# Half of one batch's x turned by VectorE and SBUF transfers instead of TensorE, the last tile in three pieces, a new order of the work

## The chip, the cores and the metric

The kernel runs on one core of a Trainium2 chip. The metric is the device time of one execution in microseconds (us), as the median of several runs. Beside it stands one execution taken by the hardware profiler, with its trace. Engines are called PE (TensorE; its weight loads PEld), DVE (VectorE), ACT (ScalarE), POOL (GpSimd) and SP (SyncE). DMAs are issued by SP or ACT, each in its own queue.

## What is computed

Causal attention for 4 batches of 8 heads over 768 tokens of 64 dimensions: three heads ("retrieval") see all earlier keys, five ("streaming") see the first 4 keys and a window of the last 64. The outputs of a batch's heads side by side are x (768 rows of 512), which goes through a feed-forward part with a maximum of two products.

```
scores = scale * q @ k.T, masked per head (full causal, or sink + window)
x      = softmax(scores) @ v                    # (4*768, 512)
g      = maximum(x @ w1, x @ w2)                # d_ff 1024
out    = g @ w_out                              # (3072, 512), float32
```

## The kernel before

The maximum is taken as relu(x·(w1−w2)) + x·w2, so that x needs one product with w12 = w1−w2 ("up"), and the output is x·(w2·w_out) plus relu(..)·w_out ("down"). The products with constant weights are made once at the start.

Attention goes by pairs of heads: 4 pairs a batch, 16 in all, numbered n. For a pair SP loads q, k and v (L478, L489); POOL casts them to bf16 (L423); q and k are turned by DVE in 32x32 squares (L566; the first pairs by PE, L552). PE makes scores (`ps`, L626), ACT takes their exponential (`at`, L643), DVE multiplies by a mask (L665), PE makes the weighted sums (`po`, L687), and DVE divides by the sum and writes x (L702, L704). x of one batch is 768 rows in 6 blocks of 128; "half" 0 is the first three blocks and half 1 the others.

Before the feed-forward part x has to be turned so that its 512 columns lie on partitions (`xt`). There are two ways. For batches 0, 1 and 2 (counting from 0), PE turns 12 blocks of 128x128 a half into a bank of PSUM (`px`, L720), and ACT or DVE copies them out (`take_x`, L748). For batch 3 (`SQUARES_FROM`, L364), DVE turns all 32x32 squares of a half in one instruction (`turn_x_squares`, L730, into `xs`), and 16 DMAs a half from SBUF to SBUF put the squares where they belong (`regroup_x`, L742); SP issues 8 of them and ACT 8.

The feed-forward part of a batch runs in two groups of three blocks: 8 "ups" of 4 matmuls (`ph`, L761), whose relu is taken by ACT (L772) or DVE (L774), then 3 "downs" of 12 matmuls (`pout`, L788), copied out (L421 on ACT, L423 on DVE) and stored (L836). The last tile of all is split in two column halves of 256 (`down_columns`, L803; `give_columns`, L815): the first is copied out by DVE and stored by SP, the second is copied and stored by ACT.

The order of the instructions on every engine is set before the program runs. A planner (`Order.plan`) has all operations with a cost and what they depend on, and plays them through. PE takes from lists in a fixed priority: x transposes (TX), scores (S), weighted sums (W), turns of q and k (TQ), feed-forward (F), products of weights (P) and, until 33 us, empty matmuls that keep PE busy (D, L903). Inside F the order is fixed: all of a batch's group 0, then group 1, then the next batch. The other engines and SP's queue take, of what is ready, the operation of the lowest rank: loads have rank 0, copies out of PSUM and late stores −1, attention of pair n about n, and `regroup_x` of batch 3 has n plus 4 for half 1. A list of seeds (`SEEDS`, `vary`) shifts the ranks of a few operations at random for each seed; PE's operations are not shifted.

Of the kernel before, what the change touches and what calls it, by code (L numbers as in the profile page):

```python
# [12 lines left out]
F32 = mybir.dt.float32  # L13
# [3 lines left out]
ACT = mybir.ActivationFunctionType  # L17
# [93 lines left out]
def heads_of(slots):  # L111
# [17 lines left out]
    130124, 130127, 130134, 130135, 130145, 130154, 130184, 130208, 130320, 130381, 130399, 130452,  # L129
    130492, 130575, 130609, 130687, 130849, 131260, 131273, 131785, 131855, 131967, 132048, 132807,  # L130
    220218, 220306, 220334, 220390, 220446, 220561, 220818, 222814, 223249, 223552, 223658, 223665,
)


class Op:


    def __init__(self, engine, cost, emit, deps=(), rank=0, tail=0.12, bank=False, issue=0.55, by="SP", single=False, port=False, shy=False):
        self.cost = cost if isinstance(cost, dict) else {engine: cost}
        self.engine, self.emit, self.rank, self.tail = engine, emit, rank, tail  # L140
        self.deps, self.bank = [d for d in deps if d is not None], bank
        self.issue, self.by, self.single, self.port, self.shy = issue, by, single, port, shy
        self.end, self.ready, self.users = None, 0.0, []
        self.behind, self.followers = None, []


class Order:
# [44 lines left out]
    def vary(self, seeds):  # L192

        self.link()
        movable = [o for o in self.ops if o.engine != "PE"]
        for seed in seeds:
            rng = random.Random(seed)
            for o in rng.sample(movable, rng.choice((1, 2, 4, 8, 20))):
                o.shift = o.shift + rng.gauss(0, 2.0) if rng.random() < 0.8 else 0.0
# [149 lines left out]
def tile_paired_heads(tc, q, k, v, w1, w2, wo, out, qkf, vf, tab, idle, heads):  # L349

    nc = tc.nc
    B, H, S, D = q.shape
# [8 lines left out]
    GTILES = GT // 128  # L361
    scale = 1.0 / float(D) ** 0.5
    ident, smask, causal = tab[:, 0:128], tab[:, 128:896], tab[:, 896:1024]
    TURNED, ANY_CASTS, SQUARES_FROM = 5, HP, B - 1  # L364
    RANKS, W_RANK = 1.0, 2.0
    FRONT = "B00 B01 B02 B03 B04 A0 L10 L11 w0 L12 w1 B10 B11 B12 B13 B14 A1 w2 w3 o0 o1 o2 o3"
    FIRST_LANDS, FIRST_TAKES = (6.0, 8.5, 12.1), (2.45, 2.55, 3.5)
# [45 lines left out]
    T = {}  # L413

    def in_bank(shape, dtype, name):

        return banks[order.bank].tile(shape, dtype, tag="b", name=name)
# [305 lines left out]
    def turn_x_squares(b, half):  # L723


        def emit(_):
            if half == 0:
                T["xs", b] = xs_pool.tile([128, NB, d_model], BF16, tag="xs", name="xs")
            rows = slice(3 * half, 3 * half + 3)
            nc.vector.transpose(  # L730
                T["xs", b][:, rows].rearrange("p i f -> p (i f)"),
                T["x", b][:, rows].rearrange("p i h d -> p (i h d)"),
            )
        return emit
# [55 lines left out]
                )  # L790
        return emit

    def down_columns(b, i, side):
        tg, ti = divmod(i, GTILES)
        cols = slice(d_model // 2 * side, d_model // 2 * side + d_model // 2)

        def emit(_):
            pout, g = in_bank([128, d_model // 2], F32, "pout"), T["g", b, tg]
            T["pout", b, i, side] = pout
            steps = [(xts[b % len(xts)][:, i, kc, :], w2o[:, kc, cols]) for kc in range(KC)]  # L800
            steps += [(g[:, fc, ti * 128:(ti + 1) * 128], wob[:, fc, cols]) for fc in range(FC)]
            for e, (lhsT, rhs) in enumerate(steps):
                nc.tensor.matmul(  # L803
                    pout, lhsT=lhsT, rhs=rhs, start=(e == 0), stop=(e == len(steps) - 1)
                )
        return emit

    def give_columns(b, i, side):
        cols = slice(d_model // 2 * side, d_model // 2 * side + d_model // 2)
        r0 = b * S + i * 128  # L810

        def emit(e):
            ot = outp.tile([128, d_model // 2], F32, tag="half", name="ot")
            copy(e, ot, T["pout", b, i, side])
            dma["ACT" if e == "ACT" else "SP"].dma_start(out=out[r0:r0 + 128, cols], in_=ot)  # L815
        return emit


# [94 lines left out]
    def prepare_w(c, rank):  # L913
        loaded = load(W_TAKES[c][0], load_w2(c), tail=W_TAKES[c][1])
        old, frees = take("qn")
        T["w1f", c] = slot("qn")[:, 0:KC * 256].rearrange("p (c f) -> p c f", c=KC)
        o = load(W_TAKES[c][2], load_w1(c), old, tail=W_TAKES[c][3])
        for two in range(2):
            subs[c, two] = op(
                None, {"DVE": 0.69, "POOL": 1.27}, subtract(c, two), [o, loaded], rank=rank, port=True, shy=True,  # L920
            )
            frees.append(subs[c, two])
        cast = op(None, {"DVE": 0.7, "POOL": 1.05}, cast_w2(c), [loaded], rank=rank, port=True)
        w2_casts.append(cast)
        ev = op(None, {"DVE": 0.69, "ACT": 1.05}, take_w2(c), rank=rank)
        ev.deps = [pe("P", 0.6, turn_w2(c), [cast], bank=ev)]
        w2t_ops.append(ev)

    def rank_of(n, part):
# [111 lines left out]
    def weigh(n, half, rank):  # L1041
        b, p = divmod(n, HP)
        mine = [x for x in tiles if used(n, x, half) and x in mask_ops]
        if (p, half) == (0, 0):
            done_with["x", b] = take("x")
        norm = op("DVE", 0.97, normalise(n, half), [*done_with["x", b][0]], rank=rank)
        for x in mine:
            w = pe(
                "W", len(used(n, x, half)) * 0.031 + 0.03,
                weighted(n, x, half, x == mine[0], x == mine[-1]),  # L1050
                [*mask_ops[x], *v_ready[n]], bank=norm if x == mine[0] else False,
            )
            frees_at[x].append(w)
        norm.deps.append(w)
        norms[b, half].append(norm)
        done_with["v", n][1].append(w)
        if (p, half) == (HP - 1, 0):
            done_with["xt", b] = take("xt")
        if p == HP - 1 and b >= SQUARES_FROM:
            if half == 0:  # L1060
                done_with["xs", b] = take("xs")
            o = op("DVE", 1.78, turn_x_squares(b, half), [*norms[b, half], *done_with["xs", b][0]], rank=n)
            done_with["x", b][1].append(o)
            turned.setdefault(b, []).append(o)
            whole = b < B - 1
            if half == 1 or not whole:
                rows = slice(0 if whole else 3 * half, 3 * half + 3)
                moved = [
                    op(
                        "DMA", 0.5 if whole else 0.25, regroup_x(b, rows, g, a),  # L1070
                        [*turned[b], *done_with["xt", b][0]], rank=n + 4 * half, issue=0.66,
                        by=("SP", "ACT")[a % 2], tail=1.2,
                    ) for g in range(4) for a in range(4)
                ]
                done_with["xs", b][1].extend(moved)
                for h in (0, 1) if whole else (half,):
                    x_ready[b, h] += moved
        elif p == HP - 1:
            for blocks in ((0, 1), (2,)) if half == 0 else ((3, 4), (5,)):
                m = len(blocks)  # L1080
                ev = op(None, {"DVE": 0.1 + 0.29 * m, "ACT": 0.2 + 0.4 * m}, take_x(b, blocks), rank=-1)
                o = pe("TX", 0.24 * m, turn_x(b, blocks), norms[b, half], bank=ev)
                ev.deps = [o, *done_with["xt", b][0]]
                done_with["x", b][1].append(o)
                x_ready[b, half].append(ev)
# [70 lines left out]
    def downs(b, tg):  # L1156
        for i in range(tg * GTILES, tg * GTILES + GTILES):
            if (b, i) == (B - 1, NB - 1):
                for side in range(2):
                    ev = op("DVE" if side == 0 else "ACT", 0.4, give_columns(b, i, side), rank=-1)  # L1160
                    ev.deps = [pe(
                        "F", 1.3, down_columns(b, i, side), [*w2o_ops, *relus[b, tg]], bank=ev
                    )]
                continue
            old, frees = take("ot") if b >= PARKED else ([*subs.values(), *w2_casts], [])
            ev = op(None, {"DVE": 0.68, "ACT": 0.6}, take_out(b, i), old, rank=-1)
            for part in range(3):
                o = pe(
                    "F", 0.87, down(b, i, part), [*w2o_ops, *(relus[b, tg] if part else ())],
                    bank=ev if part == 0 else False,  # L1170
                )
            ev.deps = [o, *ev.deps]
            done_with["xt", b][1].append(o)
            frees.append(op("DMA", 0.66, store(b, i), [ev], rank=N if b < PARKED else -1))
# [589 lines left out]
```

## Time and profile before

| | us |
|---|---|
| median of 3 runs | 183.93 |
| the 3 runs | 181.79, 183.93, 184.63 |
| the profiled execution | 181.13 |
| its span (first to last instruction) | 179.3 |
| PE busy | 171.5 |
| DVE busy | 113.5 |
| ACT busy | 110.7 |
| POOL busy | 59.2 |

The span is what the views below divide; some 1.8 us of the profiled execution lie outside it. Busy times overlap each other. The granted clock of TensorE is 0.999 over the span. A wait in these views is named by the semaphore that came last.

### The profile page before, as it was taken

The page shows a single profiled execution, that of the slowest core. Times are in us where ns is not written, and L with a number is a line of the kernel's source. Part 1 is how long each engine was busy: PE and PEld are TensorE (multiplying, and loading weights), DVE is VectorE, ACT ScalarE, POOL GpSimd, SP SyncE. Part 2 cuts the span into 40 slices and gives each one's busy share as a digit, 9 for nine tenths or more (in the row PEclk, how much of TensorE's full clock was granted, in tenths as well). Part 3 has the DMA queues.
Part 4 walks back from the last instruction along what each step waited for, and adds up shares of the span by engine and source line. Part 5 has one row for each costly group of instructions (what it writes and reads, how often), then busy time and mean ns, then how long its engine had stood idle before and what let it go on. Part 6 is the DMA issues. An engine that isn't in the chain of part 4 may idle for free.

```text
span 179.3 us, 4746 instructions
## 1 busy us (share of the span) xinstructions
PE 171.5 (96%) x1682; PEld 96.9 (54%) x1682; DVE 113.5 (63%) x270; ACT 110.7 (62%) x168; POOL 59.2 (33%) x98
## 2 busy tenths in 40 slices
PE   6899999999999999999999999999999999999990
PEld 1265665666455554556555656556555545545560
DVE  2578999871474899997979999999559530000000
ACT  3388999786767377598674896978634005426410
POOL 2244254704265655446545437535000000000000
PEclk9999999999999999999999999999999999999999
DMA  5999999989799899799897998999712668122032
GB/s 166 312 260 347 232 293 385 349 267 253 126 194 196 136 207 192 119 202 202 131 199 147 174 168 147 167 193 400 272 58 69 111 72 180 41 89 90 0 117 75
DMA packets 120675, 32.90 MB, mean 184 GB/s; under 512 B 107587, under 2 KB 116547, under 8 KB 120643
## 3 DMA queue, kind: packets, MB, share of 16 engines
q1 hardware_dynamic: 113954, 31.73, 76.4%
q10 hardware_dynamic: 6688, 0.79, 3.0%
q8 instruction: 15, 0.25, 0.6%
q14 instruction: 18, 0.14, 0.3%
HBM read 25.43 MB, written 6.29 MB: 177 GB/s over the span
## 4 chain that ended last, share of the span: by engine, by line
PE 77%; DMA 8%; DVE 7%; ACT 2%; issue 2%; POOL 1%; SPq 1%; POOLq 0%
PE pout L788 29%; PE ph L761 23%; PE ps L626 8%; PE po L687 6%; DMA w2f<-in_moe_w_dram 4%; PE po L868 4%; DMA qkf<-in_k_dram 4%; DVE at L665 2%; PE px L720 2%; DVE x L704 2%; ACT at L643 2%; PE ps L600 2%; PE pout L803 1%; DVE qk L566 1%; PE pt L552 1%
## 5 line engine op out<-in xcount | busy, mean ns | idle before, releaser
L643 ACT ACTIVATE at<-ps 128x1024 bf16<-128x1024 f32 (+2 forms) x64 | 59.5, 979 | 12.5 <-PE ps L626 9.4
L788 PE MATMUL pout<-wob,g 128*128 128x512 bf16 x184 | 45.2, 379 | 0.0
L761 PE MATMUL ph<-xt,w 128*128 128x384 bf16 x256 | 44.7, 326 | 0.0
L423 POOL CAST qb<-qkf 128x768 bf16<-128x768 f32 (+1 forms) x40 | 25.1, 643 | 35.1 <-DMA qkf<-in_k_dram 16.7
L761 PEld LDWEIGHTS <-w 128*128 128x128 bf16 x256 | 24.1, 98 | 15.6 <-issue 0.4
L772 ACT ACTIVATE g<-ph 128x384 bf16<-128x384 f32 x55 | 26.6, 492 | 8.8 <-PE ph L761 8.1
L665 DVE TENSOR_TENSOR at<-at,tab 128x1024 bf16<-128x1024 bf16 (+5 forms) x45 | 26.2, 609 | 8.8 <-ACT at L643 8.6
L788 PEld LDWEIGHTS <-g 128*128 128x128 bf16 x184 | 16.8, 98 | 18.5 <-issue 0.2
L704 DVE TENSOR_TENSOR x<-po,rez 128x192 f32 x64 | 22.9, 357 | 2.2
L788 PE MATMUL pout<-w2o,xt 128*128 128x512 bf16 x92 | 23.7, 379 | 0.0
L421 ACT COPY ot<-pout 128x512 f32<-128x512 f32 (+1 forms) x10 | 5.6, 563 | 27.5 <-PE pout L788 15.0
L687 PEld LDWEIGHTS <-at 128*128 128x128 bf16 x477 | 18.2, 98 | 6.4 <-issue 0.6
L626 PE MATMUL ps<-qk 64*128 64x128 bf16 (+2 forms) x307 | 21.2, 234 | 0.0
L566 DVE STREAM_TRANSPOSE qk<-qb 128x768 bf16<-128x768 bf16 x22 | 21.2, 966 | 0.0
L423 DVE COPY ot<-pout 128x512 f32<-128x512 f32 (+1 forms) x3 | 1.8, 603 | 30.5 <-PE pout L803 26.5
L687 PE MATMUL po<-vb,at 128*128 128x65 bf16 x387 | 20.7, 194 | 0.3 <-DVE at L665 0.3
L423 POOL CAST vb<-vf 128x768 bf16<-128x768 f32 (+1 forms) x18 | 12.2, 688 | 21.6 <-DMA vf<-in_v_dram 15.0
L626 PEld LDWEIGHTS <-qk 64*128 64x128 bf16 x307 | 11.6, 94 | 12.9 <-issue 9.6
L423 POOL COPY vx<-vb 64x650 bf16<-64x650 bf16 (+3 forms) x24 | 15.1, 632 | 1.7 <-DVE vb L423 0.5
L788 PEld LDWEIGHTS <-xt 128*128 128x128 bf16 x92 | 8.3, 98 | 8.7
L626 PE MATMUL ps<-qk,kx 64*128 64x128 bf16 x91 | 9.2, 216 | 0.1
L702 DVE RECIPROCAL rez<-po 128x6 f32<-128x6 f32 x32 | 5.9, 186 | 5.0 <-PE po L687 4.9
(67 smaller groups left out, 144.9 us busy)
## 6 DMA issues: line engine op xcount, KB each, us to landing
vf<-in_v_dram SPq DMA_DIRECT2D x24, 192.0 KB, 3.1
qkf<-in_q_dram SPq DMA_DIRECT2D x44, 96.0 KB, 3.4
qkf<-in_k_dram SPq DMA_DIRECT2D x44, 96.0 KB, 2.6
out_dram<-ot SPq DMA_DIRECT2D x11, 256.0 KB, 2.4
w2f<-in_moe_w_dram SPq DMA_DIRECT2D x4, 512.0 KB, 7.9
qkf<-in_moe_w_dram SPq DMA_DIRECT2D x4, 512.0 KB, 8.4
qkf<-in_moe_w_out_dram SPq DMA_DIRECT2D x4, 512.0 KB, 5.3
out_dram<-w2f SPq DMA_DIRECT2D x8, 256.0 KB, 3.5
```

The costliest lines, as they stand in the source:

```text
L423: eng[e].tensor_copy(out=out, in_=in_)
L566: nc.vector.transpose(T["qk", n][:, t], T["qb", n, 0][:, t])
L626: nc.tensor.matmul(ps[:, bank, e * 128:(e + wide) * 128], lhsT=lhsT, rhs=qk[rows, 0, i * 128:(i + wide) * 128], start=bank not in begun, s ...
L643: nc.scalar.activation(out=at[:, 0:len(w), 0:w[0]], in_=T["ps", n, t][:, 0:len(w), 0:w[0]], func=ACT.Exp, scale=scale,)
L665: eng[e].tensor_tensor(out=at, in0=at, in1=tbl, op=ALU.mult)
L687: nc.tensor.matmul(po[:, hh, b[-1] - 3 * half, :], lhsT=at[:, bank, e * 128:(e + 1) * 128], rhs=rhs, start=first and (bank, hh, e, b) == m ...
L702: nc.vector.reciprocal(out=rez, in_=po[:, :, :, D])
L704: nc.vector.tensor_tensor(out=T["x", b][:, 3 * half:3 * half + 3, bass.ds(heads[PLACES[n][hh]], 1), :], in0=po[:, hh, :, 0:D].unsqueeze(2) ...
L761: nc.tensor.matmul(ph, lhsT=w12[:, kc, fc * 128:(fc + 1) * 128], rhs=xts[b % len(xts)][:, 3 * tg:3 * tg + 3, kc, :], start=(kc == 0), stop ...
L772: nc.scalar.activation(out=g[:, fc, :], in_=ph, func=ACT.Relu)
L788: nc.tensor.matmul(pout, lhsT=lhsT, rhs=rhs, start=(e == 0), stop=(e == len(steps) - 1))
L868: nc.tensor.matmul(T["po2", kc], lhsT=w2t[:, fc, kc * 128:(kc + 1) * 128], rhs=wob[:, fc, :], start=(fc == 0), stop=(fc == FC - 1),)
```

## The change

The second half of batch 2 is turned in the way of batch 3: by DVE's squares and 16 DMAs. Those DMAs get rank −2, ahead of every load, copy and store, and all but the first of them are exempt from the seeds' shifts (`fixed`). The last tile's columns are made in three pieces, of 256, 128 and 128; DVE copies the first two and ACT the third, and SP issues all three stores. 30 seeds are added, and two costs in the planner (of `turn_w2` and of the regrouping DMAs) and the flag `fixed` feed the planner, so the order of the work on all engines is made anew.

```diff
@@ SEEDS
+    310092, 310174, 310178, 310206, 310265, 310282, 310350, 310385, 310535, 310648, 310677, 311155,
+    210002, 210008, 210033, 210047, 210079, 210081, 210089, 210160, 210255, 210282, 210367, 210423,
+    210770, 210861, 210874, 211140, 211669, 212024, 212690, 810963,
@@ Order.vary
-        movable = [o for o in self.ops if o.engine != "PE"]
+        movable = [o for o in self.ops if o.engine != "PE" and not o.fixed]
@@ tile_paired_heads
-    TURNED, ANY_CASTS, SQUARES_FROM = 5, HP, B - 1
+    TURNED, ANY_CASTS = 5, HP
+    SQUARES = ((B - 2, 1), (B - 1, 0), (B - 1, 1))
@@ turn_x_squares
-            if half == 0:
+            if ("xs", b) not in T:
@@ down_columns
-    def down_columns(b, i, side):
+    def down_columns(b, i, cols):
...
-            pout, g = in_bank([128, d_model // 2], F32, "pout"), T["g", b, tg]
+            pout, g = in_bank([128, cols.stop - cols.start], F32, "pout"), T["g", b, tg]
@@ give_columns
-            ot = outp.tile([128, d_model // 2], F32, tag="half", name="ot")
-            copy(e, ot, T["pout", b, i, side])
-            dma["ACT" if e == "ACT" else "SP"].dma_start(out=out[r0:r0 + 128, cols], in_=ot)
+            ot = outp.tile([128, d_model // 2], F32, tag="half", name="ot")[:, 0:cols.stop - cols.start]
+            copy(e, ot, T["pout", b, i, cols.start])
+            nc.sync.dma_start(out=out[r0:r0 + 128, cols], in_=ot)
@@ prepare_w
-        ev.deps = [pe("P", 0.6, turn_w2(c), [cast], bank=ev)]
+        ev.deps = [pe("P", 0.47, turn_w2(c), [cast], bank=ev)]
@@ weigh
-        if p == HP - 1 and b >= SQUARES_FROM:
-            if half == 0:
+        if p == HP - 1 and (b, half) in SQUARES:
+            if b not in turned:
                 done_with["xs", b] = take("xs")
             o = op("DVE", 1.78, turn_x_squares(b, half), [*norms[b, half], *done_with["xs", b][0]], rank=n)
...
-                        "DMA", 0.5 if whole else 0.25, regroup_x(b, rows, g, a),
-                        [*turned[b], *done_with["xt", b][0]], rank=n + 4 * half, issue=0.66,
-                        by=("SP", "ACT")[a % 2], tail=1.2,
+            moved = [
+                op(
+                    "DMA", 0.25, regroup_x(b, slice(3 * half, 3 * half + 3), g, a),
+                    [o, *done_with["xt", b][0]], rank=-2 if b < B - 1 else n + 4 * half, issue=0.66,
+                    by=("SP", "ACT")[a % 2], tail=1.2, fixed=b < B - 1 and g + a > 0,
+                ) for g in range(4) for a in range(4)
+            ]
@@ downs
-                for side in range(2):
-                    ev = op("DVE" if side == 0 else "ACT", 0.4, give_columns(b, i, side), rank=-1)
+                for first, m in ((0, 256), (256, 128), (384, 128)):
+                    cols = slice(first, first + m)
+                    ev = op(
+                        "DVE" if first < 384 else "ACT", 0.3, give_columns(b, i, cols), rank=-1,
+                        fixed=first == 256,
+                    )
                     ev.deps = [pe(
-                        "F", 1.3, down_columns(b, i, side), [*w2o_ops, *relus[b, tg]], bank=ev
+                        "F", m / 197, down_columns(b, i, cols), [*w2o_ops, *relus[b, tg]], bank=ev
                     )]
```

## The prediction, made before the changed kernel was run

> **What bounds the kernel now.** I read the page first, then busy times by stretches, then the chain of waits, then the single operations that the change touches. The page says that PE is busy nearly all the time:
>
> ```profile
> PE 171.5 (96%) x1682; PEld 96.9 (54%) x1682; DVE 113.5 (63%) x270; ACT 110.7 (62%) x168; POOL 59.2 (33%) x98
> ```
>
> That is an average, so I ask where PE is not busy. In the busy times by stretches the columns are: the stretch, its length, then the busy time of PE, PEld, DVE, ACT and POOL, the granted clock, the share of the DMA engines and GB/s.
>
> ```profile
> 40.00:50.00 10.00, 10.00 (x75) 5.39 (x75) 3.48 (x6) 6.35 (x12) 3.60 (x5) 1.00 0.98 196
> ...
> 65.00:72.00 7.00, 6.58 (x82) 3.59 (x81) 6.90 (x14) 4.65 (x6) 4.12 (x6) 1.00 1.09 189
> ...
> 112.00:120.00 8.00, 8.00 (x107) 4.66 (x101) 7.77 (x17) 6.39 (x8) 3.88 (x6) 1.00 0.90 161
> 120.00:130.00 10.00, 10.00 (x107) 5.89 (x106) 7.73 (x19) 7.79 (x13) 2.94 (x4) 1.00 0.91 335
> ...
> 136.00:150.00 14.00, 14.00 (x76) 7.29 (x75) 6.64 (x9) 2.41 (x6) 0.00 (x0) 1.00 0.61 89
> 150.00:165.00 15.00, 15.00 (x82) 7.87 (x81) 0.00 (x0) 7.31 (x16) 0.00 (x0) 1.00 0.29 94
> ```
>
> From 40 us to the last matmul PE is without gaps but for 0.42 us before 72 us (and 0.05 us around 106 to 112). So every microsecond of PE work taken out there is a microsecond of time, as long as nothing else comes too late. The reader should also see that DVE has 0.23 us free from 112 to 120 us, ACT 1.6 us there and 2.2 us in the next ten, and that the DMA engines are at 0.9: this is where the new work goes. The chain of waits (start, length, what) names the three places that the change touches:
>
> ```profile
> 110.66 0.37 DVE x L704
> 111.06 0.37 DVE x L704
> ...
> 112.42 0.78 PE px L720 x12
> ...
> 149.15 5.20 PE ph L761 x32
> ...
> 172.50 2.63 PE pout L803 x24
> 175.15 0.37 ACT ot L421
> ```
>
> At 112.42 stand the 12 transposes of batch 2's second half; at 149.15 begin the ups of batch 3; at 172.50 the last tile.
>
> **What the change takes away and adds.**
>
> *PE.* The 12 transposes go: 0.78 us by the chain. PE's list is full on both sides of them, so this is a gain of 0.78.
>
> *Last tile.* 24 matmuls of 256 columns take 2.63 us, 0.11 each. Now 12 of these (1.31) and 24 of 128 columns. Bounds for one of these: half of 0.11, so 1.31 together and no change; or, as the nearest row of 128 columns with a new weight each, the transposes, 0.78/12 = 0.065, so 1.56 and +0.24. I take +0.12, the middle: neither row is the same operation.
>
> *The end.* The last piece's copy falls from 256 columns to 128. ACT's copies of 512 and 256 columns average 585 and 372 ns, so 128 columns should take 372 − (585 − 372)/2 = 265 ns: −0.11. The last store goes from ACT's queue to SP's:
>
> ```profile
> 174.29 0.33 SPq L815 DMA_DIRECT2D out_dram<-ot  x1
> ...
> 175.55 0.38 ACTq L815 DMA_DIRECT2D out_dram<-ot  x1
> ```
>
> The list of DMA issues gives 3.1 us to landing for SP's half and 2.2 for ACT's. With 2.2 on SP and half the bytes, the end follows the store as now, and there is more to win: the sequencers' records have ACT's last drain at 178.46 and SP's at 178.06 though SP waited for both stores, so ACT, which leaves its program only after issuing at 175.55 to 175.93, is last by 0.4. Freed of that issue it is not. With 3.1 the end is 0.9 later. Bounds for the move −0.4 and +0.9; I take −0.4, since SP's third store has nothing in front of it: its second comes about 0.65 us earlier (12 matmuls of 128 columns) and an issue takes 0.33. With the copy: −0.5.
>
> *DVE.* One more transpose of squares, 1.75 us, and one copy out of `px` less (0.39, at 113.78; ACT's went with 1.02 at 113.30). So +1.36 on an engine with 0.23 free: masks, k turns and norms of the last pairs come that much later. PE covers it with feed-forward work in stock: groups (2,0) and (2,1) alone are 2 × 13 us. Without that cover it would cost 1.36.
>
> *DMAs.* 16 more, of 24 KB. This is how batch 3's went (ns minimum/median/maximum of an issue):
>
> ```profile
> L742 ACTq DMA_DIRECT2D xt<-xs x16: 593/636/1502, 136.8 to 148.7; - x16
> L742 SPq DMA_DIRECT2D xt<-xs x16: 585/620/1183, 136.9 to 150.3; - x16
> ```
>
> On SP 8 × 0.62 = 5.0 us, and rank −2 puts them ahead of the last pair's k loads (114.09 to 117.55) and v loads (117.80 to 118.78) and of the parked stores (118.88 to 126.6, which nobody awaits). The k that POOL cast by 120.43 was turned by DVE at 124.36, so 3.9 of the 5.0 are hidden and 1.1 lies inside DVE's own 1.36. The v cast, done at 122.49, has its mixed copies done by 124.29 and the last pair's sums come after 130: hidden. On ACT 8 × 0.636 = 5.1 us stand ahead of exponentials and copies out. The PSUM of scores frees later, so attention comes later; in exchange ACT's idle time in 112 to 130 (3.8) and the 1.02 saved can take it up, 4.8 in all. Attention's end thus moves by 5.1 + 1.36 − 4.8 = 1.7 us at the median issue time.
>
> *Who is late next.* Batch 3's x. The eighth DMAs of its half 0 are issued at 143.22 (ACT) and 143.70 (SP); with 2.1 us to landing (median of this row) x is there at 145.8. PE needs it at 149.15, or 148.4 without the transposes. Slack 2.6 against a delay of 1.7: no stall, cost 0. Its half 1 is needed only at 162.12 and issued by 150.9.
>
> *The transfers themselves.* ACT's queue, 16 such DMAs and one table, took 3.0% of 16 engines' 179.3 us, so 5.4 us of all engines for the half that is added. That falls where they are 0.9 busy. The rows cannot say whether a loaded ring stretches the issue; the bounds are the row's own, 0.59 and 1.50 us. I take the median, which most of the 32 are near.
>
> *The order.* New seeds shift everything on ACT, DVE, POOL and SP. What PE could still win after 9 us: waits of 0.3, 0.3 and 0.2 us in the list of waits, and three empty matmuls between 11 and 16 us (0.65 by the chain); in all 1.45. What it could lose has no row. I take −0.3, as most of the gaps hang on loads at the start that the diff leaves as they are.
>
> Sum: −0.78 + 0.12 − 0.5 − 0.3 = −1.46 us. The profiled execution had 181.13, so 179.7 there. It ran 2.8 us under the median of 183.93, and the trace cannot say where a slower run loses them; I carry the difference over: 183.93 − 1.46 = 182.5.
>
> **Rivals.**
>
> *Batch 3's x comes late* (slower). If each ACT issue under load takes the row's maximum, 8 × 1.50 = 12.0 us, attention ends 12.0 + 1.36 − 4.8 = 8.6 later, 6.0 over the slack, and PE stands still before the ups of batch 3: 182.5 + 6.0 = 188.5. To be over 2% slower (187.6) the stall must reach 5.1, an issue of 1.4 us. For it: DMA share 0.90 and 0.91 in the two stretches, two load issues of 2.05 and 1.81 us (105.58, 114.60), and a wait of ACT of 10.5 us for these DMAs in batch 3. Against: batch 3's ran at 0.61 and only one ACT issue of 16 was over 0.75; the neighbours of those two load issues took 0.32 to 0.72.
> *The last pair's loads come late* (slower, though within 2%). The 5.4 us that the added DMAs take of all engines come on top of SP's 5.0 for the loads issued behind them: 10.4 later, less the 3.9 hidden 6.5, and 3.9 over the slack: 186.4. For it: the 0.90 again. Against: at 0.9 a tenth of the engines' time, and the parked stores, which can wait, stand between. The Trainium skill has this as a rule that speaks against the change (DMA: Bandwidth & Descriptors, "Issuing engines are not separate DMA queues"): DMAs begun by different engines run on the same 16 DMA engines and interleave, and a second issuer saves issue time alone. By that rule the time would be 186.4, not 182.5; no row of this trace has loads and such DMAs together.
>
> *The new order pays.* All 1.45 us of gaps, and fewer changes between kinds of PE work: four matmuls of 512 columns take 0.86 us when others follow and 0.97 before scores (114.64), so 0.1 a change; ten fewer are 1.0. 182.5 + 0.3 − 2.45 = 180.3, about the bound of 2%. Against: PE's priorities are unchanged, and a change is due to what is ready.
>
> *The change does not act as it says:* the saved PE time is lost at once, because the ups of batch 3 are fixed by x and not by PE. Then only the end counts, 183.93 − 0.5 = 183.4. The slack of 2.6 speaks against it.
>
> **Chances.** My forecast 0.50, x late by ACT 0.20, the loads late 0.10, the order pays 0.15, no PE gain 0.05. The bound of 2%, about what a measurement of this kernel can tell from no change (its runs lie 1.6% apart), is 180.25 and 187.6. Faster: about half of the case in which the order pays (0.08) and a fifth of the forecast's, by the scatter of runs (0.10), 0.18. Slower: four fifths of x late by ACT (0.16), a third of the loads' case (0.03), and what an order can lose that no row shows (0.05), 0.24. Within: 0.58. The likeliest case's own range is 181.2 (the gaps gone) to 184.2 (SP's slower landing, +0.24 on PE, no gain by order). The range over all, 180.0 to 188.6, reaches to both rivals' full prices (180.3 and 188.5) and leaves out what goes beyond them, about 1 in 10 on each side.
>
> **What would show it.** In the profile after: `px` x60 in place of x72; a third transpose of squares near 112 us with 24 issues a queue; ACT issues of about 0.64 us there (over 1.4: first rival); no idle time of PE before the ups of batch 3, and their start some 0.5 to 1.1 earlier than 149.15; 24 narrow matmuls in 1.3 to 1.56 us; from the last matmul to the end of the span 3.7 us in place of 4.2. I am wrong if PE waits between 112 and 150 us, if the start before 40 us moves by more than 1 us, or if the third store takes 3 us to land.

## The result, and the profile after

| | before | after |
|---|---|---|
| median of six runs, us | 183.1 | 190.26 |
| lowest and highest | 181.74, 184.63 | 189.93, 190.7 |
| the profiled execution | 181.13 | 190.7 |
| its span | 179.3 | 188.9 |
| granted clock over the span | 0.999 | 0.977 |

The ratio is 1.0405, with a 95% interval of 1.0363 to 1.0447: slower by 4%, and 7.8 us over the forecast of 182.5. (The forecast started from the 183.93 of three runs; over six, the kernel before takes 183.1. So the 7.8 are 7.2 lost, the 1.46 that were forecast and not won, less that 0.8.) Line numbers after are 4 to 5 higher than before: q and k are loaded at L483, v at L494, the squares are at L735, the regrouping DMAs at L747, the ups at L766, relu on ACT at L777 and on DVE at L779, the downs at L793, the last tile at L807.

The page's first line and its list of waits (engine, line and operation, what it waited for; total us, times, longest) show a PE that stands still for longer than anywhere before:

```profile
PE 171.9 (91%) x1662; PEld 97.4 (52%) x1682; DVE 114.8 (61%) x271; ACT 108.7 (58%) x167; POOL 61.7 (33%) x98
```

```profile
PE ph L766 <- DVE g L779: 4.9, 1, 4.9
...
SPq L483 <- DMA xt<-xs: 10.9, 4, 8.9
```

PE's busy time is what it was (171.9 against 171.5), its share fell from 96% to 91%. PE waited 4.9 us for a relu of DVE. (It also waited 1.0 us at 90.9 and at 97.3 us, ahead of all that follows here.) The second line is odder: SP, about to issue loads of q and k (L483), waited 8.9 us for a regrouping DMA, which has nothing to do with q or k. The timeline of SP's queue (start, length, what) shows where:

```profile
105.13 0.98 SPq L494 DMA_DIRECT2D vf<-in_v_dram  x2
115.22 3.67 SPq L483 DMA_DIRECT2D qkf<-in_q_dram  x4
119.62 2.03 SPq L483 DMA_DIRECT2D qkf<-in_k_dram  x4
...
135.04 6.44 SPq L747 DMA_DIRECT2D xt<-xs  x8
```

From 106.1 to 115.2 SP issues nothing. Then come the loads of pair 14; those of the last pair follow from 123.13. In the kernel before, the q loads of these two pairs were issued from 103.69 and from 111.38 on:

```profile
103.69 3.94 SPq L478 DMA_DIRECT2D qkf<-in_q_dram  x4
111.38 2.46 SPq L478 DMA_DIRECT2D qkf<-in_q_dram  x4
```

SP's own eight new regroups are not in the way: they come at 135.04, behind all loads and nine parked stores. The eight of ACT are another matter:

```profile
113.02 6.53 ACTq L747 DMA_DIRECT2D xt<-xs  x8
```

DVE's squares of batch 2 end at 113.0, ACT issues the first regroup at 113.02, and some 2 us later, about when it has landed, SP goes on. The trace's records of the DMA issues name the reason. In this program each DMA raises a completion counter (a semaphore), and there are eight of these for SP's queue and ACT's together (numbers 100, 102, 103, 105, 107, 108, 109 and 115), taken in turn in the order in which the built program lists the DMAs. A DMA is issued only when the DMA before it on its counter has landed; the records of all 14 traces of this case have no exception. ACT's eight regroups stand in that list among SP's loads. The first of them, issued at 113.02, has counter 109 and lands at 115.10; the load that stands eight DMAs behind it in the list has counter 109 too, and is the one that SP issues at 115.22. So SP's load waits until DVE has made the squares, ACT has issued and the transfer has landed.

The chain of waits (start, length, what) follows it from the squares to PE:

```profile
111.31 1.37 DVE xs L735
...
113.81 0.62 ACTq L747
114.47 0.63 ACTq L747
115.14 0.63 ACTq L747
...
116.11 3.38 DMA xt<-xs
119.62 0.32 SPq L483
...
121.27 2.45 DMA qkf<-in_k_dram
123.87 0.84 POOL qb L428
124.73 0.99 DVE qk L571
...
126.75 0.48 DVE g L779
127.27 1.44 PE ph L766 x4
```

Loads, POOL's cast, DVE's turn, and behind that turn on DVE the relu that frees the bank PE wants. The busy times by stretches (columns as in the prediction) show what the pause costs (the clock is the third figure from the end):

```profile
115.00:122.00 7.00, 6.55 (x67) 3.73 (x67) 1.44 (x4) 2.41 (x4) 0.79 (x1) 1.00 0.79 113
122.00:125.00 3.00, 0.41 (x5) 0.23 (x3) 1.25 (x2) 1.17 (x3) 0.86 (x2) 1.00 1.11 214
125.00:127.00 2.00, 0.00 (x0) 0.00 (x0) 1.93 (x5) 0.00 (x0) 0.74 (x1) 0.64 0.95 147
127.00:132.00 5.00, 4.73 (x33) 2.33 (x33) 2.75 (x7) 2.40 (x4) 3.46 (x5) 0.50 1.06 227
132.00:134.00 2.00, 1.95 (x10) 0.93 (x9) 2.00 (x3) 1.50 (x3) 1.84 (x2) 0.91 1.06 405
```

PE first lives on feed-forward work in stock, runs dry at 122.4, and its clock falls to 0.50 some 3 us later. It stays there for 5 us of work: four ups take 1.44 us instead of 0.65. So 4.9 us of idling cost about 2.5 more (5.1 us at half speed). At 121.5 us PE was still 0.7 us ahead of before: that is by how much the fourth of batch 2's first eight ups starts earlier. The seventh starts 7.35 us later than before, the second group 9.2, batch 3's first up also 9.2 (its weight load at 157.99 against 148.77) and the last tile 9.7. So PE falls back by 9.9 us between 121.5 us and the second group at 145: 4.9 us are the pause, 2.5 the clock, and the rest, about 2.5, is by my estimate no loss but attention work that the new order puts between these two groups. (In the last run with the new order, in which PE has no gap there, it goes from 1.3 us ahead of before to 1.3 behind at the same place.)

### The profile page after: what moved, and what is told of

Same layout as the page of the kernel before. It is cut to its first block, busy times and chain, and to the rows that moved or that the text cites. A ratio compares the mean times of both kernels' runs of the same rounds, so it can differ in the third digit from the quotient of the medians.

```text
span 188.9 us, 4752 instructions
## 1 busy us (share of the span) xinstructions
PE 171.9 (91%) x1662; PEld 97.4 (52%) x1682; DVE 114.8 (61%) x271; ACT 108.7 (58%) x167; POOL 61.7 (33%) x98
## 4 chain that ended last, share of the span: by engine, by line
PE 45%; SPq 17%; DMA 16%; DVE 8%; issue 7%; POOL 2%; ACT 1%; ACTq 1%; POOLq 0%
PE ph L766 15%; PE pout L793 15%; SPq L483 13%; DMA qkf<-in_k_dram 6%; DMA qkf<-in_q_dram 5%; PE ps L631 5%; PE po L692 4%; SPq L494 3%; DMA xt<-xs 3%; DVE x L709 2%; DMA out_dram<-ot 2%; DVE at L670 2%; PE ps L605 1%; PE pout L807 1%; POOL qb L428 1%
## 5 line engine op out<-in xcount | busy, mean ns | idle before, releaser
L766 PE MATMUL ph<-xt,w 128*128 128x384 bf16 x256 | 46.8, 334 | 5.7 <-DVE g L779 4.9
L793 PE MATMUL pout<-wob,g 128*128 128x512 bf16 x177 | 43.4, 379 | 0.5 <-issue 0.3
L777 ACT ACTIVATE g<-ph 128x384 bf16<-128x384 f32 x56 | 26.7, 499 | 24.3 <-PE ph L766 12.2
L428 POOL CAST qb<-qkf 128x768 bf16<-128x768 f32 (+1 forms) x40 | 25.8, 661 | 44.6 <-DMA qkf<-in_q_dram 21.6
L766 PEld LDWEIGHTS <-w 128*128 128x128 bf16 x256 | 24.3, 99 | 22.8 <-issue 8.0
L670 DVE TENSOR_TENSOR at<-at,tab 128x1024 bf16<-128x1024 bf16 (+5 forms) x45 | 24.6, 570 | 4.9 <-ACT at L648 4.8
L793 PEld LDWEIGHTS <-g 128*128 128x128 bf16 x184 | 16.8, 98 | 18.1
L793 PE MATMUL pout<-w2o,xt 128*128 128x512 bf16 x85 | 23.1, 379 | 0.6 <-issue 0.2
L428 DVE COPY ot<-pout 128x512 f32<-128x512 f32 (+2 forms) x6 | 3.5, 578 | 29.4 <-PE pout L807 23.6
L428 POOL CAST vb<-vf 128x768 bf16<-128x768 f32 (+1 forms) x18 | 13.0, 735 | 21.5 <-DMA vf<-in_v_dram 18.9
L793 PEld LDWEIGHTS <-xt 128*128 128x128 bf16 x92 | 8.5, 98 | 9.2
L426 ACT COPY ot<-pout 128x512 f32<-128x512 f32 (+1 forms) x8 | 4.4, 545 | 14.9 <-PE pout L793 11.0
```

Source lines behind the costliest of these rows:

```text
L428: eng[e].tensor_copy(out=out, in_=in_)
L670: eng[e].tensor_tensor(out=at, in0=at, in1=tbl, op=ALU.mult)
L766: nc.tensor.matmul(ph, lhsT=w12[:, kc, fc * 128:(fc + 1) * 128], rhs=xts[b % len(xts)][:, 3 * tg:3 * tg + 3, kc, :], start=(kc == 0), stop ...
L777: nc.scalar.activation(out=g[:, fc, :], in_=ph, func=ACT.Relu)
L793: nc.tensor.matmul(pout, lhsT=lhsT, rhs=rhs, start=(e == 0), stop=(e == len(steps) - 1))
```

## The experiments

The theory: the shared counters tie SP's loads to ACT's regroups, so the loss hangs on where ACT's DMAs stand in the program's list, and not on the squares, on the bytes or on ACT's issue time. The rivals: ACT is blocked by its issues, the transfers crowd the loads, or the new order is to blame. The first four runs were compared with the kernel before at 183.71 us, the next four at 183.47, then 183.44, 183.43 twice, and 183.7. Edits are excerpts, against the kernel after unless the text says otherwise.

### All sixteen regroups issued by SP

```diff
-            o.emit(e)
+            o.emit("SP" if o.batch == 2 else e)
```

> The changed kernel with the same planned order on every engine, but the eight regrouping DMAs of batch 2 that ACT issued are issued by SP, beside SP's own eight. Theory 'shared counters': DMAs of both queues count on the same eight completion semaphores in turn, so SP's loads of the pair before the last stood behind ACT's regrouping and waited some 9 us; with no regrouping on ACT the wait is gone: no idle PE from 120 to 127 us, clock 1.0 there, 190.3 - 4.9 - 2.6 = 182.8 us (up to 184.5 if SP's sixteen come late). Rival 'transfers': the 16 transfers load the 16 DMA engines and delay the loads; the transfers are all there, so 188 to 190. Rival 'order': the new order of all engines is at fault: 190.

Measured: 183.99 us (182.44 to 186.72), ratio 1.0048 (0.9998 to 1.0099). SP no longer waits among its loads, and with that wait seven eighths of the loss are gone (4.05% became 0.5%): same squares, same bytes, same planned order. The time is inside the forecast's 182.8 to 184.5. What is left shows in the list of waits of this run (its profiled execution, 185.3, is 1.3 over its median):

```profile
PE ph L766 <- DMA xt<-xs: 2.7, 1, 2.7
```

SP's sixteen come in a row from 125.74 to 137.1, behind nine parked stores, and x of batch 2 is late.

### ACT's eight moved behind the loads

```diff
+        late = [s for s in steps if s[0].batch == 2 and s[1] == "ACT"]
+        steps = [s for s in steps if s not in late]
+        at = [k for k, s in enumerate(steps) if s[1] == "ACT" and k > 700][12]
+        steps[at + 1:at + 1] = late
```

> The changed kernel with ACT's eight regrouping issues of batch 2 moved later in ACT's order, behind SP's last loads in the built program's order. Theory 'shared counters': no load waits, so 182.5 to 184.5 us, with PE without idle time from 120 to 127. Rival 'ACT's issue time' (my prediction's rival: 8 issues hold ACT up by 5 us or more): ACT still issues all eight while attention runs, so 187 to 190. Rival 'order': 190.

Measured: 188.45 us (186.96 to 188.94), ratio 1.0284 (1.0194 to 1.0374). The loads go out without a wait, as the theory has it, and PE is busy from 120 to 130 us (9.90 of 10). But the time is not won: the forecast of 182.5 to 184.5 missed, and 188.45 is what the rival by ACT's issue time gave (187 to 190). One wait of PE and the timeline of ACT say why:

```profile
PE po L696 <- ACT at L652: 4.5, 1, 4.5
```

```profile
128.66 0.59 ACT L430 COPY ot<-pout 128x512 f32<-128x512 f32 x1 [0.72 <-PE pout L797]
128.66 5.44 ACTq L751 DMA_DIRECT2D xt<-xs  x8
134.20 1.94 ACT L652 ACTIVATE at<-ps 128x1024 bf16<-128x1024 f32 x2 [4.96 <-DMA xt<-xs]
```

Eight issues at 0.68 us stand ahead of the next two exponentials, and PE, whose stock is used up by then, waits 4.5 us for these; behind the pause it runs at half clock for 3.4 us. So the issue time, which the kernel after hides, costs its full price where no other work covers it. It is a second way to lose, not the one of the kernel after.

### Tiny DMAs in ACT's places

SP issues all sixteen as in the first run; ACT issues eight DMAs of 16 rows of 64 bytes, read from the squares and used by nobody, where its regroups stood.

```diff
+            if o.batch == 2 and e == "ACT":
+                self.tiny()
+            o.emit("SP" if o.batch == 2 else e)
...
+        nc.scalar.dma_start(out=small_to[:, j], in_=T["xs", 2][0:16, 5, 32 * j:32 * j + 32])
```

> As the first, SP issues all 16, but where ACT's eight were ACT issues eight DMAs of 16 rows of 64 bytes from the same turned tile to a scratch tile that nobody reads. Theory 'shared counters': eight small DMAs are enough to hold SP's loads: 188 to 191 us, with a wait of SP of about 9 us for them near 106 us. Rival 'transfers': 1 KB each is no load on the engines, so the time is that of the first run, 182 to 184.5.

Measured: 193.23 us (191.44 to 194.34), ratio 1.0529 (1.0434 to 1.0623), with these waits:

```profile
SPq L485 <- DMA small_to<-xs: 11.5, 2, 9.5
...
PE ph L768 <- DVE g L781: 4.9, 1, 4.9
PE ph L768 <- DMA xt<-xs: 3.1, 1, 3.1
```

1 KB a DMA holds SP as long as 24 KB did (9.5 against 8.9 us), and PE waits the same 4.9 us for the same relu. The volume of the transfers is not the cause. ACT's issue time is not told apart here, as ACT still issues eight; the run with one tiny DMA does that. The time is 2.2 us over the forecast of 188 to 191, which had left out the late x of the first run: the 3.1 us, and 6.8 us at half clock behind them.

### The change without batch 2's squares

```diff
-    SQUARES = ((B - 2, 1), (B - 1, 0), (B - 1, 1))
+    SQUARES = ((B - 1, 0), (B - 1, 1))
```

> The changed kernel without the squares of batch 2 (PE turns its second half as before); the added seeds, the planner's costs and the last tile in three pieces stay. Theory 'shared counters': 182 to 184 us, some 0.5 us of it won at the end. Rival 'order': the new seeds are at fault, so 187 to 190.

Measured: 183.29 us (181.85 to 184.19), ratio 1.0005 (0.9963 to 1.0047). New seeds, new costs and three pieces, without the squares, are neither a gain nor a loss that shows; the 0.5 us that were expected at the end are not seen.

### Sixteen by SP, ahead of the nine parked stores

```diff
+        late = [s for s in steps if s[0].batch == 2]
+        first = steps.index(late[0])
+        parked = [s for s in steps[:first] if s[1] == "SP"][-9:]
+        steps = [s for s in steps if s not in parked]
+        at = steps.index(late[-1]) + 1
+        steps[at:at] = parked
+            o.emit("SP" if o.batch == 2 else e)
```

> The change with all 16 regroups of batch 2 issued by SP, and these 16 put ahead of the nine parked stores, directly behind the last pair's loads. Theory (the loss is the shared completion counters; what was left over in the variant with the issues on SP was that they came behind nine stores, 5.7 us): the last pairs' loads go out without a wait as in the run of before (pair 15 near 112 to 119 us), the sixteen take about 11.4 us behind them, x is there near 134, the second group of batch 2 waits for no DMA (2.7 us less than the variant with stores first), and the clock stays at 1.0 up to 150. Then the change's gains, transposes and end, show: 182.3 us, between 181.5 and 183, ratio to before 0.990 to 1.000. Rival (SP issuing sixteen in a row loads the DMA engines so that the last loads or the stores are late): 184 or more, with PE idle in 130 to 150.

Measured: 183.19 us (182.38 to 188.31), ratio 1.002 (0.9978 to 1.0062). The loads and batch 2's x are in time, and PE is without a gap to 136 us. The forecast of 182.3 missed, because the wait moved on by one batch. The chain of waits of this run:

```profile
137.62 1.77 DVE xs L741
139.41 0.74 ACTq L753
...
140.64 3.42 DMA xt<-xs
144.08 0.59 ACTq L753
...
148.42 2.17 DMA xt<-xs
150.62 5.36 PE ph L772 x32
```

Batch 3's regroups go out on both queues behind fifteen stores of 256 KB (130.40 to 139.1), and the first three take 3.4 to 4.5 us to land, against a median of 2.1 in the kernel before. SP's second regroup (143.92) has the counter of ACT's first (139.41, landed at 143.90) and so waits 3.8 us; ACT's sixth waits for ACT's own second (140.64, landed at 144.06). PE waits 1.6 us for batch 3's x.

### One tiny DMA

The kernel of the last section, with a single DMA of 16 x 64 bytes by ACT where its first regroup stood. In the program's list it takes a counter just ahead of pair 13's v loads; the next user of that counter is the second k load of pair 14, eight DMAs on.

```diff
+            if o.batch == 2 and e == "ACT":
+                self.tiny()
...
+            nc.scalar.dma_start(out=small_to, in_=T["xs", 2][0:16, 5, 0:32])
```

> As the run with SP's sixteen ahead of the stores, with one DMA of 16 x 64 bytes more, issued by ACT behind batch 2's squares, where its first regroup stood. Theory of the counters (eight in turn over both queues): not the next load waits now but the one that has the same counter eight DMAs later, the second k load of pair 14. So SP issues v of pair 13, four q and one k of pair 14 (up to about 109 us) and then stands until the tiny DMA has landed, about 115: a wait of 5 to 7 us at k, none at q. The last loads end near 124.5, about 5 us earlier than in the run of after; PE's wait for relu is 1 us or less instead of 4.9; time 182.5 to 184.5. Rival (any DMA on ACT's queue holds SP's, or a DMA behind the squares delays the next load whatever its counter): the first q load waits to 115 and the time is 190 or more. Rival (the volume of ACT's transfers): no wait at all.

Measured: 188.88 us (187.66 to 189.42), ratio 1.0298 (1.0228 to 1.0368). The wait, and SP's timeline:

```profile
SPq L491 <- DMA small_to<-xs: 5.6, 1, 5.6
```

```profile
105.72 0.98 SPq L502 DMA_DIRECT2D vf<-in_v_dram  x2
106.94 3.58 SPq L491 DMA_DIRECT2D qkf<-in_q_dram  x4
110.77 7.57 SPq L491 DMA_DIRECT2D qkf<-in_k_dram  x4
118.60 0.98 SPq L502 DMA_DIRECT2D vf<-in_v_dram  x2
```

Place and length are as forecast: v, then all four q and one k without a wait, then one wait of 5.6 us before the second k load. The tiny DMA (issued at 115.16) has counter 109 and lands at 116.87; the second k load has counter 109 and is issued at 116.89. A DMA on ACT thus does not hold SP's queue as such, it holds one counter. ACT's issue time is no rival here: it is 0.65 us. The time was missed by 4.4 us. The last loads ended at 126.9 and not 124.5: in this execution SP was later before the tiny DMA (q of pair 14 at 106.94, against 105.61 and 104.05 in the first and the fifth run), and the wait ended near 117 instead of 115. PE then waited 1.7, 1.8 and 2.6 us in all for relu, x and masks, where I had counted on one wait of 1. One DMA of 1 KB costs 5.7 us here (188.88 against 183.19).

### Batch 2's squares alone, in the old order

The kernel before with the new `SQUARES`, the regroups by half and their rank, but the old seeds and two pieces. "Old order" means the old seeds: with other operations in it, the planner makes a plan that is not that of before.

```diff
-    310092, 310174, 310178, 310206, 310265, 310282, 310350, 310385, 310535, 310648, 310677, 311155,
...
-                for first, m in ((0, 256), (256, 128), (384, 128)):
+                for side in range(2):
```

> The kernel before with batch 2's second half through squares alone, the old order's seeds and the old two pieces. Here ACT's eight have their counters ahead of the first k load of pair 14 and behind three of its q loads. Theory of the counters: q of pair 14 goes out as before (to about 108 us), the k loads wait for ACT's second regroup, landed near 115.5 to 116; pair 15's loads then end near 126 instead of 118.8 (before) or 129.4 (after). PE waits less than in after, some 1 to 3 us; time 184 to 187.5. Rival (the new order of the seeds is what makes the squares slow): as before, 183 to 183.5. Rival (issues or volume, wherever they stand): as after, 190.

Measured: 193.24 us (192.66 to 194.19), ratio 1.0544 (1.0481 to 1.0608). Again the wait is where the counters put it, and the waits and the timeline show it:

```profile
SPq L480 <- DMA xt<-xs: 6.5, 2, 6.1
...
PE ph L763 <- DVE g L776: 6.8, 1, 6.8
```

```profile
106.68 4.03 SPq L480 DMA_DIRECT2D qkf<-in_q_dram  x4
117.01 3.61 SPq L480 DMA_DIRECT2D qkf<-in_k_dram  x4
```

The q loads go out with no wait for a regroup (3 us later than in before), the k loads wait 6.1 us, and the first of them has the counter of ACT's second regroup, as forecast. But I forecast 184 to 187.5 from the later end of the loads alone. PE ran dry from 121.0 us, waited 1.3 and then 6.8 us, and then worked for 5.1 us at half the clock. The k loads come 2.6 us earlier than in the kernel after (117.01 against 119.62), and yet PE goes on 2.7 us later (129.99 against 127.27): the relu that it waits for stands on DVE behind one more turn of q and k (at 128.51), whose cast stands on POOL behind a v load. So the size of the stall is set by what the order happens to put behind the late loads, and not by their delay alone. That the old seeds lose more (9.8 us) than the new ones (7.2) clears the new seeds as the cause of the loss.

### Three pieces alone

The edit is shown against the kernel before.

```diff
-                for side in range(2):
-                    ev = op("DVE" if side == 0 else "ACT", 0.4, give_columns(b, i, side), rank=-1)
+                for first, m in ((0, 256), (256, 128), (384, 128)):
...
+                        "DVE" if first < 384 else "ACT", 0.3, give_columns(b, i, cols), rank=-1,
```

> The kernel before with only the last tile's three pieces, all stored by SP. If the end gains what the trace of after shows (last matmul to span's end 4.0 instead of 4.2 us) the time is 0.2 us below before, ratio 0.997 to 1.000, which five rounds may just not tell apart; if the prediction's 0.5 us were right, 0.997. If SP's own issue of two narrow stores one behind the other costs more than ACT's issue of one did, it is 1.000 to 1.003.

Measured: 183.25 us (181.8 to 185.45), ratio 1.0007 (0.9972 to 1.0042). The end of the last matmul to the end of the span is 3.9 us here, 4.2 before, 4.0 after; a gain of 0.2 or 0.3 us lies inside the interval.

### Old order, sixteen by SP, three pieces

The fifth run's edit of the steps on the kernel of the squares alone, with the three pieces.

> The kernel before with its old order, with batch 2's second half through squares, all 16 of its regroups issued by SP directly behind the last loads and ahead of nine parked stores, and with the three pieces of the last tile: the change without its new order and without an issue on ACT ahead of batch 3. In the run with the new order and SP's sixteen first, x of batch 2 was in time and 1.6 us were lost on batch 3's x, whose squares ended at 141.0 us there and at 138.5 in before. If that was the new order's doing (attention's end put behind more of the batch-2 work), then here the squares of batch 3 end at 138.5 or earlier, no wait for x is left, and the gains show: 0.78 us of transposes and 0.2 us of the end, 182.2 to 182.6 us, ratio 0.994 to 0.998. If the wait for batch 3's x came from the stores that now stand ahead of its regroups on SP, it is here too: 183.5 to 185, with PE waiting 1 to 2 us near 150.

Measured: 184.05 us (182.58 to 185.98), ratio 1.0018 (0.9982 to 1.0054). The loss is gone here too, but no gain came of it; the time is that of the forecast's second case (183.5 to 185), in which the stores are the cause. The profiled execution, 1.9 us over the median, has PE waiting 1.4 us for batch 3's x, with SP's second regroup at 147.09 behind a store that waited 1.9 us for a counter of a regroup. That pointed to the stores, which the next two runs take out of the way.

### The twelve parked stores behind batch 3's regroups

```diff
+        parked = [s for s in steps if s[1] == "SP" and s[0].rank == 16]
+        steps = [s for s in steps if s not in parked]
+        at = max(k for k, s in enumerate(steps) if s[0].batch) + 1
+        steps[at:at] = parked
+            o.emit("SP" if o.batch == 2 else e)
```

In the old order:

> As the last run (old order, SP's sixteen, three pieces), with the twelve parked stores of batches 0 and 1 put behind batch 3's regroups on SP, so that none stands ahead of them. Theory: in the last run PE waited 1.4 us for batch 3's x because SP issued its first regroup only at 142.8 and its second at 147.1, behind stores and a store's wait of 1.9 us for a counter that a regroup of ACT held; with the stores gone from there SP's first regroups go out right behind the squares, the wait for x near 150 is gone, and the change's gain shows: 182.3 to 183.0, ratio 0.993 to 1.000. Rival (the wait is ACT's own issue rate of 0.7 us for its regroups, or other jitter of the loads): PE waits 1 us or more for x as before and the time stays within 0.3 us of 184.0 on the same chip. Rival (stores put last on SP come late and hold the end): the last matmul to the span's end is over 4.5 us.

In the change's order:

> The same with the change's own order (all of the change but ACT's eight issues, and the twelve parked stores behind batch 3's regroups). In the run with the new order and nine stores moved, PE waited 1.6 us for batch 3's x, whose squares end 5.2 us behind the start of batch 2's second group there, against 2.7 in before. If the stores are the cause, the wait goes and the time is 182 to 182.8, ratio 0.992 to 0.999; if the late squares are, 1 us or more of the wait stays and it is 183 to 184, ratio 0.999 to 1.005.

Measured, old order: 183.99 us (181.42 to 185.54), ratio 0.9978 (0.9931 to 1.0026). Measured, the change's order: 180.93 us (180.52 to 182.54), ratio 0.9864 (0.9823 to 0.9906). In both, PE no longer waits for batch 3's x; the ups of batch 3 follow the downs before them without a gap. The old order missed its forecast in us (182.3 to 183.0), though its ratio is inside the forecast's; the change's order is better than its forecast (182 to 182.8). In the change's order PE has no gap at all from 112 us on, though the execution in the trace, 182.54, is the slowest of its seven and 1.6 over their median:

```profile
112.00:120.00 8.00, 8.00 (x73) 4.24 (x72) 6.73 (x14) 2.75 (x5) 4.87 (x7) 1.00 0.91 159
120.00:130.00 10.00, 10.00 (x113) 5.91 (x110) 9.18 (x20) 8.24 (x15) 4.21 (x5) 1.00 0.67 106
130.00:136.00 6.00, 6.00 (x65) 3.16 (x62) 4.84 (x14) 3.85 (x5) 0.00 (x0) 1.00 0.38 73
136.00:150.00 14.00, 14.00 (x93) 7.52 (x92) 7.31 (x12) 3.81 (x8) 0.00 (x0) 1.00 0.49 90
```

This version is faster than both kernels, by 1.4% against before. In the old order the wait went and the time hardly did. So the stores were the cause of that wait. Why the old order wins nothing by it is in part in its trace: before 36 us PE stands still there for 0.7 and 1.1 us behind DVE, and then runs at half clock for 3.4 us. The kernel before shows neither; the change's order has one pause of 1.2 us there and no half clock. From the last matmul to the end of the span it is 4.5 us in the old order and 4.3 in the change's, against 4.2 before: the rival "stores put last hold the end" stands at its bound of 4.5, and nothing is won at the end.

### Control: the kernel before with the parked stores last

The same move of the stores in the kernel before.

> The kernel before with nothing of the change, only the twelve parked stores put behind batch 3's regroups on SP: the control for the two last runs. If the 1.4% that the new order won there come from the change (transposes gone, end) once its DMAs are out of the way, this is as before: 183.0 to 183.8, ratio 0.997 to 1.003. If they come from the stores' place alone, it is 181 to 182, ratio 0.986 to 0.992.

Measured: 183.34 us (182.16 to 185.94), ratio 0.999 (0.9952 to 1.0027). The stores' place alone brings nothing, and the change without its squares brought nothing either (1.0005, with the stores in their old place). So the 1.4% are the change's, once its DMAs are out of the way. How much of it is the squares and how much the new order with the stores last is not shown: that order without batch 2's squares was not run.

## Why the prediction was wrong

*What bounds the kernel* stood: PE's work decided, and where PE stood still the time went. A wait of PE between 112 and 150 us, one of the named signs of being wrong, is what came (122.4 to 127.3).

*PE.* The transposes went (`px` x60 in place of x72). That the 0.78 us are a gain could not show in the kernel after. With the DMAs out of the way the change as a whole gained 2.5 us (1.36% of 183.4), more than the 1.16 that the sum has without the order's share; what the rest is due to was not separated, and the 0.78 were not measured by themselves.

*Last tile.* The 36 matmuls took 2.66 us against 2.63 for the 24: +0.03 in place of the +0.12 taken, close to the lower bound of no change.

*The end.* ACT's copy of 128 columns took 265 ns, as worked out. The third store was issued at 185.21, right behind its copy, but its issue took 1.28 us and not 0.33, and it landed after 2.7 us and not 2.2 (the median of the two narrow stores is 2.9; 3 was one of the named signs of being wrong). From last matmul to the span's end it was 4.0 us instead of 3.7, so −0.2 in place of −0.5. Even that is not sure: in the fifth run and the two with the stores last it was 4.3 to 4.5, over the 4.2 of before.

*The order.* −0.3 was taken; the run without the squares, which has the three pieces too, measured 1.0005, with 0.8 us of uncertainty either way. No gain by the order alone shows.

*DVE.* The third transpose of squares stands at 111.22 and takes 1.77 us. It was hidden, as argued: in the version where nothing else is late PE has no gap from 112 us on.

*DMAs: the step that failed,* twice. First, "rank −2 puts them ahead of the last pair's k loads" is wrong. The planner lets SP issue loads ahead of time, so by the time the squares are made SP's loads and nine stores are already in its order, and rank picks only among what is still to come. SP's eight came at 135.04. In the kernel after, where all else was late too, PE did not wait for them; with all sixteen there, in the first run, PE waited 2.7 us. Second, and this is nearly the whole 7.2 us lost, the step priced the DMAs by the issue time on each queue (8 × 0.62 and 8 × 0.636) and took SP's queue and ACT's as independent. They share eight counters. The cost of ACT's eight was not the 5.1 us of issue, which at 6.5 was near enough and fell where PE still had work, but 8.9 us of SP's time in front of the loads of the last two pairs. This could have been read before the run: the issue records of the kernel before already name a counter for each DMA, the same eight on both queues.

*Who is late next.* With the loads 11.5 us late, the slack of 2.6 us at batch 3's x, worked out for a delay of 1.7, had no meaning; batch 3's first up came 9.2 later. The work in stock held PE for 16 us behind the last load in time, until 122.4, and no longer. The sum had a price for late loads among its rivals only, and no term for the clock at all, which made 2.5 us of the loss.

*The rivals.* "The last pair's loads come late" named the right victim for the wrong reason: it counted on full DMA engines and gave 186.4. The engines were emptier than before; from 105 to 115 us their share was 0.96 before (first row) and is 0.30 after (second):

```profile
105.00:115.00 10.00, 9.95 (x144) 6.04 (x142) 9.67 (x21) 8.43 (x11) 5.45 (x8) 1.00 0.96 165
105.00:115.00 10.00, 9.89 (x105) 5.70 (x105) 9.51 (x22) 6.53 (x9) 3.45 (x4) 1.00 0.30 59
```

The rule cited with it from the Trainium skill (DMA: Bandwidth & Descriptors, "Issuing engines are not separate DMA queues"), that a second issuer saves issue time alone, misses this case: here the second issuer cost time on the first, while the shared engines stood at 0.30. "Batch 3's x comes late" by slow issues of ACT did not happen: the median issue was 0.63 us and the largest of all 24 was 1.17. It would have given 188.5 for another reason than the 190.3 that came. The second run shows that such a price can be paid at another place, 4.5 us of PE's time for eight issues of normal length.

## What to carry to other kernels

Before moving a DMA or adding one on a second queue, find out which completion counter it takes and who takes it next: in this program a transfer that waits for late data blocked, eight DMAs on, the DMA with the same counter, on either queue and even at 1 KB. Price a delay of loads by the work that the consumer has in stock at that place and by what stands behind those loads on the engines in between, and add the clock: here 3.4 to 5.1 us of work at half speed behind pauses of PE of 4.5 to 6.8 us. DMAs that wait for late data did best on the queue whose remaining loads had already gone out, with the stores that nobody awaits behind them all.

## What was not expected of the hardware

The clock's steps are sharp: the traces' records of the granted clock have only 1.00 and 0.50, so a figure between them in a stretch is a mix of both. Half clock lasted 6.83 us in the kernel after (125.54 to 132.37), 3.41 in the first run, 3.42 in the second, 3.41 and 6.83 in the third, and 10.24 in the run of the squares alone: about 3.41, or two or three times that. How long a pause it takes, and how much work at half clock follows, differs. After: PE without work from 122.4 us, half clock from 125.5, work again at 127.27, so 3.1 us to fall and 5.1 us of work to rise. In the second run: no work from 130.8, half clock from 135.4, work at 135.3, full from 138.8, so 4.6 and 3.4.

The length of the pause alone does not decide. With pauses of 1.6 and 1.7 us (fifth and sixth run) the clock stayed at 1.00; with one of 2.7 us (first run) it fell; but it also fell, for 3.41 us from 35.76, in the run of the old order with the stores last, where PE had paused for 0.7 and 1.1 us only, with little work between. In the 3.41 us ahead of each of these falls PE was busy for 45% of the time or less. No run was made to find the bound.

A DMA of 1 KB, issued by ACT in 0.65 us and read by nobody, cost 5.7 us by the medians, as it held a counter that a load needed.
